# A windowed-attention and expert kernel on one core: feed-forward one slot earlier, a PSUM layout change brought forward, gates moved within their slot, and more loads requested early

## The chip, the cores and the metric

The kernel runs on one core of one Trainium2 chip. The metric is the device time of one execution in microseconds; lower is better. A profile covers one execution, and its span is some 1.7 us shorter than the time of the same execution (221.6 of 223.31). On one core there is no second die to compare with, so a run counts as slow when it is over 1.5% above the fastest run of the same kernel.

## The reference

Eight batches of 576 positions go through attention with eight heads of 64 (four with a plain window of 32 keys, four with every fourth of the last 128 keys). Then each whole batch is sent to one of eight experts, chosen from the mean of its attention output:

```python
pooled = x.mean(axis=1)
logits = pooled @ w_gate
e_idx = np.argmax(logits, axis=1)
...
h = np.maximum(x[mask] @ w1[e], 0.0)
out[mask] = gate_w[mask, None, None] * (h @ w2[e])
```

The expert of a batch, and so the address of its `w1` and `w2` (2 MB each in HBM, 1 MB each as bf16 in SBUF), is known only when all attention of that batch is done.

## The kernel before

Attention is cut into 32 slots, four to a batch. In slot t, PE transposes q or k for a later slot, finishes the attention product (AV) of slot t-1, computes the scores of slot t, and then works off some feed-forward units of an earlier batch. A batch has eight units: four of the first layer (64 matmuls of 128x288 in all, with `w1`), four of the second (32 of 128x512 in all and a tail, with `w2`). `UNITS` says how many units each slot takes:

```python
UNITS = [0] * 6 + [1] * 4 + [2] * 30
```

So the first layer of batch b >= 1 begins in slot 8 + 4b (the lag is 8 slots from the batch's first slot). The gate of batch b is emitted in slot 5 + 4b, when its last AV has been normalised. The gate computes the logits, brings the index of the expert to the POOL engine, and requests weights and later inputs:

```python
def emit_gate(b):
    ...
    nc.vector.max_with_indices(mx[:], mi[:], l_sb[:])
    e_val = nc.values_load(mi[0:1, 0:1].bitcast(I32), engines=[ET.Pool], ...)
    ...                       # three requests for w1, 512 + 256 + 256 KB as landed
    if b == 0:
        load_1(2, GO[0], "q"); load_va(2); load_qb(2)
        load_w2(e_val, w2b)
        load_qa(3); load_vb(2)
    else:
        load_vb(b + 2)
        load_w2(e_val, w2b)
        load_qa(b + 3)
    load_va(b + 3)
    load_qb(b + 3)
```

POOL issues all loads in this order; in the traces of the kernel before never more than eight of the 123 were under way at once. The stores of the output go out from SP. PSUM is laid out in two ways: an early one with two sets of AV banks, and a late one with one AV group `nd` and three banks `m`. The late one began after slot 5. The main loop, cut:

```python
for t in range(6, len(UNITS)):
    if t > 6:
        run_T(t)                       # transposes
    pre.av_a(); flush(); cur.sx()      # AV of t-1, stores, scores of t
    ...
    for i, f in enumerate(items[:k0]):
        f()
        if i == k0 // 2 and gn == 0 and 0 < gb < B:
            emit_gate(gb)              # gate in the middle of the slot
    pre.norm()
    for i, f in enumerate(items[k0:]):
        f()
```

The softmax here doesn't subtract the row's maximum and nothing guards it: scores larger than these inputs give would overflow.

## Time and profile before

| | before |
|---|---|
| time, median of the first three runs | 225.66 us |
| span of the profiled run | 221.6 us |
| PE busy | 194.9 us, 88% |
| share of the software DMA queue | 96.2% |
| gate 7 (its matmul) to the end of the span | 189.27 to 221.6, 32.3 us |

The prediction below shows the lines on which the reading of the bound rests. Where it calls PE cold, it means a slower PE as in this trace: nine transposes took 1.14 us at 33.80, 1.05 us after a wait of 2.22 us had ended, and 0.68 us at 38.42.

### The profile page before, as it was taken

To read this page: it belongs to the slowest core of one execution; us is meant where nothing else is said; L and a number is where in the kernel's file an instruction comes from. 1 tells how busy PE (TensorE), PEld (TensorE's weight loads), DVE (VectorE), ACT (ScalarE), POOL (GpSimd) and SP (SyncE) were. 2 spreads that over 40 slices of the span, in tenths; PEclk is the share of its full clock that TensorE was granted. 3 is DMA by queue.
4 is the path that set the end of the run, shared out by engine and by line. 5 is a ranking of instruction groups with operands and counts; after the bars stand their busy time and mean duration, and the time that the engine had idled before them with its cause. 6 is when DMAs were issued, how large, how long until landed. Compare 5 with 4: busy or idle time off the path is not lost.

```text
span 221.6 us, 8268 instructions
## 1 busy us (share of the span) xinstructions
PE 194.9 (88%) x3570; PEld 135.3 (61%) x3584; DVE 127.9 (58%) x364; ACT 129.9 (59%) x231; POOL 83.1 (38%) x133
## 2 busy tenths in 40 slices
PE   0687559878999999999999999999999999999992
PEld 0565457656567765776577756776577557647641
DVE  5356466657576756765676666676676455415312
ACT  2487666775657766668657665766676755232320
POOL 7974294614852182508450557027100500400000
PEclk9999999999999999999999999999999999999999
DMA  5999499999999999999999999999993699299723
GB/s 81 192 187 188 69 116 193 207 205 180 182 218 203 232 210 215 231 244 209 201 206 232 214 207 229 219 223 208 220 193 109 113 174 288 35 177 249 160 95 118
DMA packets 49925, 41.18 MB, mean 186 GB/s; under 512 B 23777, under 2 KB 38113, under 8 KB 49889
## 3 DMA queue, kind: packets, MB, share of 16 engines
q0 software_dynamic: 43440, 31.20, 96.2%
q1 hardware_dynamic: 6448, 9.46, 12.7%
q8 instruction: 28, 0.46, 0.8%
q14 instruction: 9, 0.07, 0.1%
HBM read 62.41 MB, written 9.44 MB: 324 GB/s over the span
## 4 chain that ended last, share of the span: by engine, by line
PE 60%; DMA 16%; ACT 7%; DVE 5%; issue 5%; POOL 4%; POOLq 1%; SPq 0%
PE m L612 22%; PE m L592 18%; DMA w2b<-in_moe_w_dram 7%; DMA qm<-in_q_dram 7%; PE nd L360 6%; PE m L258 4%; ACT pt L325 3%; PE m L627 3%; ACT qk L279 3%; PE m L268 3%; DMA km<-in_k_dram 3%; DVE pt L332 3%; PE ps L292 2%; DVE ht L599 2%; POOL w1b L538 1%
## 5 line engine op out<-in xcount | busy, mean ns | idle before, releaser
L592 PE MATMUL m<-xt,w1b 128*128 128x288 bf16 x512 | 68.6, 288 | 1.6 <-DVE ht L599 1.6
L592 PEld LDWEIGHTS <-w1b 128*128 128x128 bf16 x512 | 48.6, 98 | 16.3 <-issue 3.0
L612 PE MATMUL m<-w2b,ht 128*128 128x512 bf16 x242 | 56.8, 380 | 1.2 <-DMA w2b<-in_moe_w_dram 0.4
L597 ACT ACTIVATE ht<-m 128x288 bf16<-128x288 f32 x64 | 26.2, 410 | 27.3 <-PE m L592 23.8
L612 PEld LDWEIGHTS <-ht 128*128 128x128 bf16 x256 | 23.9, 98 | 28.2 <-DMA w2b<-in_moe_w_dram 0.5
L332 DVE TENSOR_TENSOR pt<-pt,mk 128x896 bf16<-128x896 bf16 x32 | 20.0, 624 | 28.8 <-ACT pt L325 28.8
L533 POOL DMA_DIRECT2D w1b<-in_moe_w_dram x9 | 6.4, 708 | 74.7 <-PE m L592 57.3
L325 ACT ACTIVATE pt<-ps 128x896 bf16<-128x896 f32 x32 | 28.9, 904 | 6.0 <-PE ps L292 6.0
L497 DVE SCALAR_TENSOR_TENSOR xt<-nd,rd 128x320 bf16<-128x320 f32 (+1 forms) x54 | 27.1, 539 | 7.5 <-ACT rd L470 7.5
L599 DVE TENSOR_SCALAR ht<-m 128x288 bf16<-128x288 f32 x64 | 27.2, 451 | 7.1 <-PE m L592 6.6
L279 ACT ACTIVATE qk<-m 128x512 bf16<-128x512 bf16 (+1 forms) x24 | 17.5, 730 | 16.6 <-PE m L258 13.3
L127 POOL DMA_DIRECT2D vm<-in_v_dram x32 | 24.2, 786 | 2.4 <-DMA qm<-in_q_dram 0.9
L276 DVE COPY qk<-m 128x640 bf16<-128x640 bf16 (+1 forms) x24 | 18.9, 786 | 6.8 <-PE m L258 4.8
L360 PEld LDWEIGHTS <-vm 64*64 64x64 bf16 x896 | 15.9, 114 | 10.7 <-issue 4.4
L470 ACT ACTIVATE rd<-lnd 128x576 f32<-128x576 f32 x32 | 21.8, 682 | 1.0
L360 PE MATMUL nd<-pt,vm 64*64 64x64 bf16 (+1 forms) x760 | 18.0, 194 | 4.3 <-DVE negm L565 2.2
L619 DVE TENSOR_SCALAR osb<-m,gbc 128x512 f32<-128x512 f32 x16 | 12.0, 751 | 16.4 <-PE m L612 16.4
L464 ACT ACTIVATE lnd<-nd 128x576 f32<-128x576 f32 x27 | 17.4, 645 | 4.5 <-PE nd L360 4.4
L292 PE MATMUL ps<-qk 64*64 64x96 bf16 (+3 forms) x608 | 16.1, 213 | 4.4 <-issue 2.0
L292 PEld LDWEIGHTS <-qk 64*64 64x64 bf16 x608 | 15.1, 118 | 4.9 <-issue 3.1
L360 PE MATMUL nd<-pt,ones 64*64 64x256 bf16 (+2 forms) x244 | 16.5, 243 | 0.2 <-issue 0.2
L617 ACT ACTIVATE osb<-m,gbc 128x512 f32<-128x512 f32 x16 | 10.9, 680 | 7.4 <-PE m L612 7.2
(73 smaller groups left out, 210.6 us busy)
## 6 DMA issues: line engine op xcount, KB each, us to landing
w2b<-in_moe_w_dram POOLq DMA_DIRECT2D x8, 1024.0 KB, 13.0
out_dram<-osb SPq DMA_DIRECT2D x32, 256.0 KB, 6.5
km<-in_k_dram POOLq DMA_DIRECT2D x16, 288.0 KB, 12.7
qm<-in_q_dram POOLq DMA_DIRECT2D x16, 288.0 KB, 12.8
w1b<-in_moe_w_dram POOLq DMA_DIRECT2D x16, 256.0 KB, 8.0
w1b<-in_moe_w_dram POOLq DMA_DIRECT2D x7, 512.0 KB, 7.6
vm<-in_v_dram POOLq DMA_DIRECT2D x8, 256.0 KB, 10.7
vm<-in_v_dram POOLq DMA_DIRECT2D x32, 64.0 KB, 8.7
```

The source lines that it names most:

```text
L127: nc.gpsimd.dma_start(out=t[:, h], in_=v[b, h, 0:512, :].rearrange("(c p) d -> p c d", p=P))
L279: nc.scalar.activation(out=ev[x][0], in_=ev[x][1], func=AF.Copy)
L292: nc.tensor.matmul(ps[half(e), a, o : o + rhs.free_size()], lhsT=lhsT, rhs=rhs, start=True, stop=True, skip_group_check=True)
L325: nc.scalar.activation(out=pt[:], in_=s["ps"][:, :, 0:NP], func=AF.Exp, scale=0.125)
L332: nc.vector.tensor_tensor(out=pt[:], in0=pt[:], in1=mk[:, g : g + 1, :].to_broadcast([P, 2, NP]), op=ALU.mult)
L360: x = nc.tensor.matmul(oo, lhsT=lhsT, rhs=rhs, start=start, stop=True, skip_group_check=True)
L470: nc.scalar.activation(out=rd[:], in_=s["lnd", n][:], func=AF.Exp, scale=-1.0)
L497: nc.vector.scalar_tensor_tensor(out=o, in0=a0, scalar=1.0, in1=a1, op0=ALU.mult, op1=ALU.mult, accum_out=s["pool"][:, w, c : c + 1],)
L592: nc.tensor.matmul(hm, lhsT=s["w1"][:, c, fc * P : (fc + 1) * P], rhs=s["xt"][:, c, cols], start=(c == 0), stop=(c == 3))
L597: nc.scalar.activation(out=o, in_=hm, func=AF.Relu)
L599: nc.vector.tensor_scalar_max(out=o, in0=hm, scalar1=0.0)
L612: nc.tensor.matmul(om, lhsT=s["ht"][:, fc, r * P : (r + 1) * P], rhs=s["w2"][:, fc, :], start=(fc == 0), stop=(fc == 7))
```

## The change

The intent is to start feed-forward one slot earlier, so that the whole takes 39 slots instead of 40. To have inputs and banks for it, the late PSUM layout starts with gate 0, and most loads of batch 2 are requested before gate 0. Later gates go to the head of their slot, since they now have one slot less. The core of the diff (the reordering of slots 3 to 5 is cut):

```diff
-UNITS = [0] * 6 + [1] * 4 + [2] * 30
+UNITS = [0] * 5 + [1] * 4 + [2] * 30
...
-    load_tiles(2)
-    load_1(2, GO[0], "k")
+    load_qa(2)
+    load_va(2)
+    load_1(2, GO[1], "k")
...
         if b == 0:
-            load_1(2, GO[0], "q")
-            load_va(2)
-            load_qb(2)
+            load_1(2, GO[1], "q")
             load_w2(e_val, w2b)
...
     emit_gate(0)
-    dve(0)
+    late()
     sl[4].sx()
...
-    for t in range(6, len(UNITS)):
+    for t in range(5, len(UNITS)):
...
+        if gn == 0 and 0 < gb < B:
+            emit_gate(gb)
         pre.av_a()
...
-        for i, f in enumerate(items[:k0]):
+        for f in items[:k0]:
             f()
-            if i == k0 // 2 and gn == 0 and 0 < gb < B:
-                emit_gate(gb)
```

More of the change, by code (lines that the diff above doesn't have):

```diff
@@ L85, in early_bank @@
         return pools["early"].tile([P, 512 if dt == F32 else 1024], dt, name=nm, tag=nm, space=PSUM)[:]
+    for x in range(2):
+        for y in range(3):
+            early_bank(x, y)
     def late():
@@ L737 @@
     dve, act = emit_T(1, a, "k", ((0, 0), (0, 1)))
-    act(0)
+    dve(0)
     act(1)
@@ L741 @@
     dve, act = emit_T(1, a, "q", ((0, 2), (0, 0)))
+    act(0)
     act(1)
     emit_gate(0)
-    dve(0)
+    late()
     sl[4].sx()
-    dve0, act0 = emit_T(1, z, "k", ((1, 1), (1, 2)))
+    run_T(4)
     sl[4].mask()
-    dve0()
-    act0()
-    sl[4].av_a()
-    sl[5].sx()
-    sl[4].av_b()
-    sl[4].ln()
-    sl[4].rd()
-    dve1, act1 = emit_T(1, z, "q", ((1, 0), (1, 1)))
-    sl[5].mask()
-    dve1()
-    act1()
-    sl[4].norm()
     emit_gate_w(0)
-    late()
     def unit(b, u):
@@ L781 @@
         items = [lambda i=i, e=e: i(e) for i, e in zip(items, engs)]
-        if t > 6:
+        gb, gn = divmod(t - 5, NSLOT)
+        if t > 5:
             run_T(t)
+        if gn == 0 and 0 < gb < B:
+            emit_gate(gb)
         pre.av_a()
@@ L786 @@
         cur.sx()
-        if t == 6:
-            run_T(t)
         if pre.on and not cur.on:
@@ L794 @@
         pre.rd()
+        if t == 5:
+            run_T(t)
         k0 = len(items) // 2
-        gb, gn = divmod(t - 5, NSLOT)
-        for i, f in enumerate(items[:k0]):
-            f()
-            if i == k0 // 2 and gn == 0 and 0 < gb < B:
-                emit_gate(gb)
+        for f in items[:k0]:
+            f()
         pre.norm()
-        for i, f in enumerate(items[k0:]):
+        for f in items[k0:]:
             f()
```

## The prediction

> **What bounds the kernel now.** I read the page's busy shares and 40 slices first, then the chain that ended last in order of time, then the timelines of PE and POOL around the two places where that chain leaves PE, and last the busy times of chosen stretches.
>
> ```profile
> PE 194.9 (88%) x3570; PEld 135.3 (61%) x3584; DVE 127.9 (58%) x364; ACT 129.9 (59%) x231; POOL 83.1 (38%) x133
> ...
> PE   0687559878999999999999999999999999999992
> ...
> DMA  5999499999999999999999999999993699299723
> ```
>
> PE is the bound from slice 12 to slice 38 and idles 26.7 us in all (221.6 - 194.9), mostly in the first 12 slices and in the last two. DMA is full nearly everywhere, with one dent near the start (the 4) and dents near the end. These are the two places the change acts on. The busy times of stretches show the first dent:
>
> ```profile
> 24.00:28.00 4.00, 1.72 (x63) 1.50 (x58) 1.99 (x7) 2.28 (x3) 1.69 (x3) 1.00 0.14 15
> 28.00:33.00 5.00, 2.74 (x110) 2.64 (x114) 3.12 (x8) 3.05 (x8) 4.60 (x9) 1.00 0.95 119
> 56.00:168.00 112.00, 108.91 (x2126) 75.24 (x2134) 73.24 (x205) 74.05 (x133) 45.16 (x68) 1.00 1.26 216
> ```
>
> The columns are PE, PEld, DVE, ACT, POOL, clock, DMA share, GB/s. From 24 to 28 us DMA moves 15 GB/s: all requested loads have landed, and nothing more is asked for until gate 0 has picked its expert. From 56 to 168 us PE is busy 108.9 of 112 us while DMA moves 216 GB/s without a hole. So the middle is bound by PE, with DMA only just keeping up.
>
> The first batch, in the timeline:
>
> ```profile
> 26.31 0.70 POOL L533 DMA_DIRECT2D w1b<-in_moe_w_dram  x1 [6.42 <-DVE qk L276]
> ...
> 32.75 0.48 PE L360 MATMUL nd<-pt,vm 64*64 64x64 bf16 x16 [2.22 <-DVE negm L565]
> ...
> 35.49 2.82 PE L592 MATMUL m<-xt,w1b 128*128 128x288 bf16 x16
> ```
>
> The first weights are requested at 26.31. PE waits 2.2 us for the single late `nd` bank group (it has to be freed by slot 4's normalisation, which ended just before `negm`), and feed-forward starts at 35.49. The chain then has four breaks, and these lines show three of them:
>
> ```profile
> 43.51 1.14 issue
> ...
> 48.93 1.98 issue
> ...
> 190.38 0.29 POOLq L527
> ...
> 193.51 15.65 DMA w2b<-in_moe_w_dram
> 209.16 0.05 issue
> 209.21 0.39 PE m L612
> ```
>
> (The fourth is a 0.41 us wait for a q load at 38.41.) The end is the important one: from the gate of batch 7, whose matmul starts at 189.27, through the expert index and the requests, to w2's landing at 209.16 is 19.9 us. PE fills all but 0.39 us of that with other work. The DMA path from gate 7 and PE are in near-perfect balance here: any work taken out of that interval uncovers the transfer.
>
> [...] a w2b load takes 13.0 us in the median and 15.65 at the end, with w1's 1 MB ahead of it. [...] The trace has an instruction queue with 28 packets and 0.46 MB, so 16 KB each, and the two "issue" stalls above are 254 PE instructions apart (counted in the program order). [...] Nine transposes take 1.14 us at 33.8 and 0.68 us at 38.4[...].
>
> **The change, part by part.**
>
> *More early loads.* q, v (with its tail) of batch 2's first head group and k of the second are requested before gate 0: 288 + 256 + 64 + 288 = 896 KB as landed, nearly 2 MB as read. At the 190 GB/s of 8 to 23 us that is 4.7 us of transfer, just the dent of 24 to 28. DMA then runs on from 24 to about 28.5, where w1b's bytes began at 28.2 before. So w1b is late by some 0.3 us, while everything after it arrives about 4.5 us sooner. The q load that PE awaited at 38.41 is one of them: -0.4 us. w2 of batch 0 landed at 48.5 and was used at 55.7, so its earlier arrival is worth nothing.
>
> *Late layout and feed-forward from slot 5.* At 32.75 PE had finished scores 0 to 5, AV 0 to 4 and the transposes up to batch 1. The new order puts the first feed-forward unit directly behind that same work. Its input is w1b's first half. From the waits of POOL's eight request slots I read that this landed between 31.8 and 33.0 (POOL could reuse the first one's slot at 31.8, the third's by 33.0). So PE, done with slot 5's work near 30.6, waits until about 32.7 for weights instead of until 32.75 for `nd`. The wait changes its name and hardly its end. From there both kernels have the same remaining PE work in another order. AV 5, scores 6 and one transpose (2.7 us cold, 32.75 to 35.48) move behind the unit (2.8 us cold): 0.
>
> *Slots 6 to 8.* PE has about 4 us a slot there, and the loop AV, ln, reciprocal, norm, next AV takes the same 3.9 us (39.02 to 42.96 before), so nothing is gained. [...] I keep the 3.1 us of stalls.
>
> *Gates at the slot's head.* With feed-forward one slot further on, the gate is half a slot earlier in its slot, so it has less cover before w1 is used: before, gate 4 at 121.95 to first use at 138.12, 16.2 us; now 16.2 less five feed-forward items (2.6) and some 0.4, 13.2. The third w1b request slot came free 12.2 to 14.0 us after gates 1 to 4. With DMA ahead by 4.5 us while PE is not, I expect landing at 9 to 12 us, no stall; w2 (before 24 us after the gate, now 25 available) neither.
>
> *The end.* Between gate 7 and w2's use there was 19.55 us of PE work (19.94 less 0.39). Moved ahead of the gate are 20 feed-forward matmuls (2.6 us). What is left is gate 0.35, second layer of batch 6 7.0, tail 1.07, first layer of batch 7 8.0, gate weight 0.4: 16.8 us. The DMA path still needs 19.9, perhaps 19.4, because the stores begin 3.4 us sooner relative to the gate and use the idle DMA before w1 moves. So 2.6 to 3.1 us of wait in place of 0.4: +2.2 to +2.7.
>
> Sum of the span: 221.6 - 0.4 + 0.3 + 2.4 = 223.9, a loss of about 1%; as a time, 225.66 x 223.9/221.6 = 228.0.
>
> **Rivals.**
> 1. *A clear gain, 1 to 2%.* Feed-forward a slot earlier, with one slot fewer, might save PE idle time at the start: [...] 3 us go away and the loss at the end is paid back, 221 span, 225. [...]
> 2. *DMA becomes the bound in the middle.* If PE does gain at the start, w1 arrives after 13.2 us and PE stalls at each batch: 0.5 to 1 us in some of them, 229 to 230. For it: 12.2 to 14.0 us before. Against: the filled dent, and DMA's queue was already draining slightly faster than PE used it.
> 3. *The extra loads delay w1b of batch 0.* They are ahead of it in the queue; were they issued late or moved slower than 190 GB/s, w1b lands at 34 to 35 and PE idles, cold, 1 to 2 us more: 229.
> 4. *PE cools at the end.* It would stand for 2.5 us before the last batch's first layer[...].
>
> **Range and chances.** The mechanisms nearly cancel; the largest sure term is the uncovered w2 (+2.4), the largest uncertain one the instruction stalls (-3 to 0). I shade the 228.0 down to 227.3 for rival 1, which has more room than 2 to 4 together. Range 223.5 to 230.0. Faster by 2% needs below 221.1, which would take a gain of over 6 us at the start: 0.06. Slower by 2% is above 230.2, which needs rivals 2 or 3 on top: 0.07.
>
> **What would show it.** Right: DMA without a dent at 24 to 28; PE's first feed-forward matmul near 32.7 and waiting for w1b; no wait for q at slot 7; two "issue" stalls of 1 to 2 us between 40 and 55; PE's work in 56 to 168 unbroken; and at the end a chain from POOL's gate read over w2b to the second layer, with 2.5 to 3 us of PE idle before batch 7's layers. Wrong: an unbroken PE from 32 to 55 (rival 1), waits for w1b in the middle (2), a first feed-forward matmul after 34 (3), or a gate 7 so much earlier that the end comes before 221.

## More of the kernel before

All profiles are of fast runs, and the times quoted for experiments are medians of the fast runs.

One more pair is needed later, from the timeline at the end: the gate's matmul, the first store of batch 6 and the first layer of batch 7 (start, length, engine, line, operation, count).

```profile
189.27 0.34 PE L520 MATMUL m<-wg_t,pooled 128*1 128x8 f32 x8
...
195.06 5.58 SPq L620 DMA_DIRECT2D out_dram<-osb  x4
...
200.52 8.00 PE L592 MATMUL m<-xt,w1b 128*128 128x288 bf16 x64
```

Gate 7 and the first use of its `w1` are 11.25 us apart, and that `w1` landed 11.1 us after the gate, so it was just in time. The stores of batch 6 begin to leave 5.8 us after the gate.

## The result

The changed kernel takes 235.0 us in the median (233.33 to 235.73, four runs) against 225.66 for the kernel before (the three fast runs, 225.33 to 227.25; the fourth, 230.69, is 2.4% above the fastest and counts as slow). The ratio is 1.036 with a 95% interval of 1.027 to 1.045: slower. In the experiments a ratio is the mean time of one kernel's fast runs over that of the other's of the same rounds, so not quite the ratio of the medians quoted; for this result the runs listed would give 1.038, within the interval. The prediction of 227.3, with 223.5 to 230.0 as range, was wrong.

First the page of the changed kernel: PE, clock and DMA in 40 slices of 5.8 us, then the group of the first layer's matmuls (busy us, mean ns, idle time in front of them).

```profile
PE   0487739869999998999899997999999999938992
PEclk9995556979999999999999999999999999997998
DMA  5999999990899999999999999999991996499123
...
L595 PE MATMUL m<-xt,w1b 128*128 128x288 bf16 x512 | 71.5, 298 | 14.5 <-DMA w1b<-in_moe_w_dram 12.1
```

In the kernel before, this group had 68.6 us busy and 1.6 us of idle time before it, none of it for `w1`. Now PE waits 12.1 us for `w1`. There is a 3 near PE's end. The dent in DMA has not gone: it has moved from slice 5 to slice 10. The stretches show it (PE, PEld, DVE, ACT, POOL, clock, DMA share, GB/s):

```profile
24.00:28.00 4.00, 2.28 (x85) 2.07 (x88) 2.24 (x10) 3.05 (x6) 2.23 (x4) 0.50 1.29 200
...
52.00:58.00 6.00, 5.95 (x123) 4.10 (x123) 3.90 (x16) 4.58 (x8) 0.98 (x2) 0.96 0.07 14
```

From 24 to 28 us DMA is full, as intended (200 GB/s, 15 before). But POOL has now issued everything gate 0 allows by 48 us, and until gate 1 has chosen an expert (its matmul at 54.62) there is nothing to ask for: 14 GB/s from 52 to 58.

The chain of waits in the middle repeats the following for batches 2 to 5 (start, length, what):

```profile
79.55 0.29 POOLq L532
...
82.07 9.45 DMA w1b<-in_moe_w_dram
91.52 0.14 issue
91.65 4.08 PE m L595 x32
```

POOL reads the index of the expert of batch 2, requests `w1`, and the first layer starts as soon as it has landed. In the kernel before the chain ran through PE here. The end:

```profile
196.50 0.34 PE L525 MATMUL m<-wg_t,pooled 128*1 128x8 f32 x8
...
198.79 0.71 POOL L538 DMA_DIRECT2D w1b<-in_moe_w_dram  x1 [18.07 <-PE m L615]
199.46 5.58 SPq L623 DMA_DIRECT2D out_dram<-osb  x4
...
209.35 9.67 PE L595 MATMUL m<-xt,w1b 128*128 128x288 bf16 x64 [4.47 <-DMA w1b<-in_moe_w_dram]
```

PE waits 4.5 us for the last `w1`, and the same 64 matmuls then take 9.67 us instead of 8.00, at a clock of 0.5 to 0.57 for the first 3 us.

**Where the 10.1 us of span went (231.7 - 221.6).** I cut at two events: the first matmul of batch 0's second layer, and gate 7. At the cuts the two kernels have done different work, so the kernel before is corrected from its own trace. At the first cut it has done one slot of attention more, 1.57 us (54.12 to 55.69), so 55.62 becomes 54.05. At gate 7 it has still to do 20 first-layer matmuls and a gate weight of batch 6, 2.9 us; with them done first, its gate 7 would stand near 192.1. This is an estimate, good to some tenths.

| part | before, corrected | after | lost |
|---|---|---|---|
| start to second layer of batch 0 | 54.05 | 55.86 | 1.8 |
| from there to gate 7 | 138.05 | 140.64 | 2.6 |
| work moved ahead of gate 7 | 192.1 - 189.27 | | 2.8 |
| gate 7 to the end | 32.35 | 35.2 | 2.85 |

The sum is 10.05. The third line was in the prediction, as 2.6 us; the other 7.2 us were not. The last two lines belong together: in this kernel the end costs 5.7 us.

### The profile page after: what moved, and what is told of

Read it like the earlier page. It is cut to its first block, busy times and chain, and to the rows that moved or that the text cites.

```text
span 231.7 us, 8254 instructions
## 1 busy us (share of the span) xinstructions
PE 196.3 (85%) x3570; PEld 136.6 (59%) x3584; DVE 128.8 (56%) x364; ACT 130.9 (57%) x230; POOL 83.2 (36%) x133
## 3 DMA queue, kind: packets, MB, share of 16 engines
q1 hardware_dynamic: 6448, 9.46, 12.7%
## 4 chain that ended last, share of the span: by engine, by line
PE 42%; DMA 30%; DVE 8%; issue 6%; ACT 6%; POOL 5%; POOLq 2%
PE m L595 24%; DMA w1b<-in_moe_w_dram 23%; PE m L615 9%; DMA vm<-in_v_dram 4%; ACT pt L330 3%; DMA qm<-in_q_dram 3%; PE m L263 3%; DVE pt L337 2%; PE nd L365 2%; ACT qk L284 2%; DVE ht L602 2%; POOL w1b L543 1%; DVE qk L281 1%; PE m L630 1%; POOLq L532 1%
## 5 line engine op out<-in xcount | busy, mean ns | idle before, releaser
L595 PE MATMUL m<-xt,w1b 128*128 128x288 bf16 x512 | 71.5, 298 | 14.5 <-DMA w1b<-in_moe_w_dram 12.1
L595 PEld LDWEIGHTS <-w1b 128*128 128x128 bf16 x512 | 50.5, 101 | 31.7 <-issue 13.0
L502 DVE SCALAR_TENSOR_TENSOR xt<-nd,rd 128x320 bf16<-128x320 f32 (+1 forms) x56 | 28.4, 544 | 7.6 <-ACT rd L475 7.6
L284 ACT ACTIVATE qk<-m 128x576 bf16<-128x576 bf16 (+1 forms) x26 | 19.0, 730 | 13.5 <-PE m L273 8.0
L281 DVE COPY qk<-m 128x576 bf16<-128x576 bf16 (+1 forms) x26 | 20.3, 782 | 9.0 <-PE m L263 8.1
L365 PE MATMUL nd<-pt,vm 64*64 64x64 bf16 (+2 forms) x784 | 18.7, 195 | 3.4 <-issue 2.0
L365 PEld LDWEIGHTS <-vm 64*64 64x64 bf16 x896 | 15.2, 112 | 8.9 <-issue 4.4
L469 ACT ACTIVATE lnd<-nd 128x576 f32<-128x576 f32 x28 | 18.0, 643 | 0.9 <-PE nd L365 0.9
L297 PE MATMUL ps<-qk 64*64 64x96 bf16 (+3 forms) x608 | 15.2, 209 | 2.7 <-issue 1.2
## 6 DMA issues: line engine op xcount, KB each, us to landing
qm<-in_q_dram POOLq DMA_DIRECT2D x16, 288.0 KB, 11.8
```

The costliest lines, as they stand in the source:

```text
L281: nc.vector.tensor_copy(out=ev[x][0], in_=ev[x][1])
L284: nc.scalar.activation(out=ev[x][0], in_=ev[x][1], func=AF.Copy)
L297: nc.tensor.matmul(ps[half(e), a, o : o + rhs.free_size()], lhsT=lhsT, rhs=rhs, start=True, stop=True, skip_group_check=True)
L365: x = nc.tensor.matmul(oo, lhsT=lhsT, rhs=rhs, start=start, stop=True, skip_group_check=True)
L502: nc.vector.scalar_tensor_tensor(out=o, in0=a0, scalar=1.0, in1=a1, op0=ALU.mult, op1=ALU.mult, accum_out=s["pool"][:, w, c : c + 1],)
L595: nc.tensor.matmul(hm, lhsT=s["w1"][:, c, fc * P : (fc + 1) * P], rhs=s["xt"][:, c, cols], start=(c == 0), stop=(c == 3))
```

## The experiments

**Theory 1** is that of cover: the work between a batch's gate and the use of its `w1` has shrunk to about the time that `w1` takes to arrive, so each gate makes PE wait. **Theory 2**: the hole at 52 to 58 us puts the whole DMA stream behind. **Theory 3**: the loss is at the start. All runs are timed against the kernel before on the same chip; the kernel before varied from 224.3 to 231.3 us in those rounds, slow runs included, so I rest on ratios of fast runs and, inside a run, on the trace.

### One slot of lag given back: a_lag8

```diff
-UNITS = [0] * 5 + [1] * 4 + [2] * 30
+UNITS = [0] * 6 + [1] * 4 + [2] * 30
```

> The changed kernel with feed-forward one slot later again (six empty slots), all else of the change kept. Theory 1 (cover): what slows the changed kernel is that w1 of a batch is used about 13 us after its gate, as long as it takes to land, so PE waits for w1 at batches 2 to 5 and 7. With a slot more of cover (some 19 us) no w1 wait is left in the middle or at the end, about 225 to 227 us, level with before. Theory 2 (DMA stream: the hole at 52 to 58 us puts the whole stream behind): waits for w1 or w2 stay, 230 us or more. Theory 3 (the start: early loads in front of the first w1 and a cold PE): about 2 us lost at the start stay, 228 to 229 us.

221.94 us, ratio 0.980 (0.969 to 0.990), on two fast runs only (222.47 and 221.41; the two slow ones took 226.75 and 226.86). No wait for `w1` or `w2` is left, and gate 7 is at 187.53.

```profile
PE   0585669979999999799999999999999999999992
...
L595 PE MATMUL m<-xt,w1b 128*128 128x288 bf16 x512 | 69.4, 291 | 2.1 <-DVE ht L602 1.8
```

With everything else of the change kept, the loss is gone; it hangs on the one slot. By itself this run doesn't separate the theories: the hole at 52 to 58 us is filled too (195 GB/s), and the wait for the first `w1` is gone, as the attention of one more slot now comes before it. The next runs do.

### Gates in the middle of the slot again: a_gatemid

```diff
-        if gn == 0 and 0 < gb < B:
-            emit_gate(gb)
         pre.av_a()
...
+            if i == k0 // 2 and gn == 0 and 0 < gb < B:
+                emit_gate(gb)
```

> The changed kernel with later gates back in the middle of their slot. Theory 1: each gate comes about 2.6 us of PE work later while w1's use stays, so each of batches 1 to 7 waits some 2 to 2.6 us longer: 15 us on top of 235, 248 to 252 us. Theories 2 and 3: the place of the gate in the slot matters little, 234 to 238 us.

264.29 us, ratio 1.164 (1.154 to 1.175): right direction, larger than theory 1 said. `w1` still lands 11.8 to 13.5 us after gates 1 to 7, and PE waits for it at every batch.

```profile
L595 PE MATMUL m<-xt,w1b 128*128 128x288 bf16 x512 | 84.1, 331 | 30.7 <-DMA w1b<-in_moe_w_dram 29.0
...
71.86 6.95 PE L595 MATMUL m<-xt,w1b 128*128 128x288 bf16 x32 [3.60 <-DMA w1b<-in_moe_w_dram]
```

The part I had left out is that PE is slower after a wait. After one of 3.60 us the next 32 matmuls take 6.95 us, where 4.08 is their time in the changed kernel (the chain line above). The group is busy for 84.1 us instead of 71.5: 12.6 us more for the same matmuls.

### Without the early loads: a_noearly

```diff
-    load_qa(2)
-    load_va(2)
-    load_1(2, GO[1], "k")
+    load_tiles(2)
+    load_1(2, GO[0], "k")
```

(and gate 0 requests the rest again, as before.)

> The changed kernel without the 2 MB of early loads (only k of batch 2 before gate 0, as in before). Theory 1: first feed-forward matmul near 32.7 instead of 34.5, then the q wait of before comes back; the w1 waits of the middle and the end stay: 232 to 235 us. Theory 2: the hole at 52 to 58 us goes, w1 lands in time in the middle, 228 us or less. Theory 3: most of the loss goes, 228 us or less.

233.99 us, ratio 1.033 (1.027 to 1.040), as theory 1 said. The hole is back at 24 to 28 us (26 GB/s), and 52 to 58 us has 171 GB/s. The first feed-forward matmul comes at 33.31, the second layer of batch 0 at 53.21, 2.65 us earlier than in the changed kernel. And yet gate 7 is at 196.63, where it was at 196.50: PE now waits for `w1` at batches 1 to 6 as well (14.8 us in all with batches 0 and 7). So what is gained at the start is taken back at the gates: theory 3 falls as the main cause. And with no hole at 52 to 58 us the waits for `w1` are still there: theory 2 falls.

### The early loads alone: b_early

The same lines of the diff, put into the kernel before.

> The kernel before with the early loads alone. Theory 1: 16 us of cover remain, so no w1 wait; first w1 lands 1 to 2 us later, but feed-forward started at 35.5 anyway, and the q wait of 0.4 us goes: 225 to 227 us, same. Theory 2: a hole in the DMA stream near 50 to 58 us and waits for w1 or w2 afterwards, 229 us or more. Theory 3: 1.5 to 2 us lost at the start, 228 us.

223.93 us, ratio 0.991 (0.980 to 1.001). The hole moves to 50 to 56 us (71 GB/s) here too, and the middle has no wait for weights after it. One wait of 0.61 us for `w1` appears at gate 7 (189.34 to 201.16, so `w1` landed 11.7 us after the gate): the kernel before had its 11.25 us of cover there with nothing to spare. A hole without waits in the middle speaks against theory 2 once more.

### The gates' place alone: b_head

The gate moved to the head of the slot in the kernel before.

> The kernel before with gates 1 to 7 at the head of their slot, alone. Theory 1: cover grows from 16.2 to some 19 us, nothing waited for w1 before, and the last w2 gets about 3 us more, so only its 0.4 us wait goes: 225 to 226.5 us, same. If the head itself cost something (a wait of PE for the gate's bank or for the pooled sums, 7 times), 1 to 3 us slower, 228 us.

225.08 us, ratio 0.991 (0.981 to 1.001); no wait for weights anywhere. The head of the slot costs nothing that can be seen.

### Weights that don't wait for the gate: a_w1free

The loads of gates 1 to 7 take a fixed expert, so POOL requests them without waiting:

```diff
+        if gn == 3 and gb + 1 < B:
+            emit_gate_loads(gb + 1, gb + 1)     # w1, w2 of expert gb + 1, same bytes, same order
```

> Wrong result on purpose: the changed kernel with the loads of gates 1 to 7 taken for a fixed expert, so that they no longer wait for the gate and follow in the queue at once. Same bytes, same order. Theory 1: no wait for w1 is left in the middle or at the end, no hole at 52 to 58 us; what stays is the late start: 225 to 228 us. If the sheer rate of DMA were the limit, waits for weights stay and the time stays above 231 us.

226.66 us, ratio 1.006 (0.995 to 1.017). Its output is wrong, which doesn't matter for the time. The sheer rate of DMA is not the limit: the same bytes in the same order need no wait when they are asked for in time. Against the changed kernel's trace the span falls by 8.9 us (231.7 to 222.8): 1.6 up to the second layer of batch 0, 1.45 in the middle (140.64 to 139.19), and 5.8 from gate 7 to the end (35.2 to 29.4). The 1.6 are not the edit's: it leaves the loads of gate 0 as they were, and gate 0 alone came 1.0 us sooner in this trace (23.45). So most of the loss is at the last gate, not in the waits of the middle, though those add up to 3.7 us (0.82, 0.86, 1.48, 0.51).

### Loads held back so that w1 goes first: a_prio and b_prio

```diff
         else:
+            load_qb(b + 2)
             load_vb(b + 2)
             load_w2(e_val, w2b)
             load_qa(b + 3)
         load_va(b + 3)
-        load_qb(b + 3)
```

> The changed kernel with the last two loads of each gate (k and q of the second head group, 576 KB) held back until the next gate's w1 has been requested. Theory 1: w1 lands some 2.5 to 3 us sooner after its gate (10 to 11 us instead of 13.3), the waits for w1 at batches 2 to 5 go, the end stays: 230 to 232 us. If the stream's rate is the limit, waits for other loads take their place, 234 us or more.

233.92 us, ratio 1.034 (1.026 to 1.042): a miss. Of the four waits for `w1` in the middle one is left (1.09 us) and a wait for `w2` joins it (0.74), yet the stretch from the second layer of batch 0 to gate 7 is as long as in the changed kernel: 140.44 us. In the middle `w1` landed 12.0 to 13.4 us after its gate, against 12.8 to 13.7, so the order of the queue is worth less than the 2.5 to 3 us that I expected. POOL now runs dry sooner (48 GB/s from 46 to 56 us), and the end, with 4.50 us of wait, is untouched.

> The kernel before with the same two loads held back. w1 had cover to spare there: theory 1 says no gain, 225 to 227 us; a loss of 1 to 3 us if DMA runs dry at gates, since the held-back loads filled it.

227.2 us, ratio 1.004 (0.995 to 1.013): no gain, as expected.

### The stores and the last w1: a_storelate

What was open by now: at the last gate nothing else is queued, and still `w1` takes 12.7 us (196.50 to 209.22). In the changed kernel the second layer of batch 6 follows right behind the gate, so its stores leave 3.0 us after it instead of 5.8. Here those stores wait until PE has begun batch 7's first layer:

```diff
-        flush()
+        hold["on"] = t in (34, 35)
+        flush()                      # does nothing while on
...
         for f in items[:k0]:
             f()
+            if t == 35 and stores:
+                flush(hold["last"])  # stores depend on that matmul
```

> The changed kernel with the six stores of batch 6 held until PE has begun batch 7's first layer, that is until w1 of batch 7 has landed. If the stores that leave at 199 to 206 us delay that w1 (12.8 us after its gate though the queue was empty), it lands some 2.5 to 3 us sooner, about 10 us after the gate, PE waits 1.5 us instead of 4.5 and does not cool, and the run is 3 to 4.5 us shorter than the changed kernel: 230 to 232 us. If those 12.8 us are the request's own path, nothing changes: 234 to 236 us.

231.95 us, ratio 1.027 (1.022 to 1.033). The timeline:

```profile
198.05 0.35 PE L525 MATMUL m<-wg_t,pooled 128*1 128x8 f32 x8
...
208.40 8.00 PE L595 MATMUL m<-xt,w1b 128*128 128x288 bf16 x64 [1.97 <-DMA w1b<-in_moe_w_dram]
```

`w1` lands 10.2 us after the gate (2.5 sooner), PE waits 1.97 us, and the layer takes 8.00 us. From gate 7 to the end it is now 31.05 us instead of 35.2: 4.15 us less, within what was expected. That gate 7 came 1.5 us later in this run (198.05) hides part of it in the time.

The packets in the two traces, counted by queue, say how. In the changed kernel, from 203.5 to 209.2 us, the queue of the loads and that of the stores moved 124 GB/s each; with the stores held back the loads alone moved 194 (203 to 208.2). The other traces agree in the main: the last `w1` landed 12.6 to 12.8 us after gate 7 where the first store left up to 3.0 us after it (the changed kernel, a_gatemid, a_noearly, a_prio, a_fill), 11.1 to 11.7 where it left after 5.8 (the kernel before, b_early, b_prio, a_lag8mid), and 10.1 to 11.8 where it left after 7.3 (a_lag8, a_lag8_again, b_head).

### PE kept busy through the wait: a_fill

Twenty matmuls of no use, into a bank that nobody reads, ahead of batch 7's first layer:

```diff
+        if t == 35:
+            fill = bank()
+            for j in range(20):
+                nc.tensor.matmul(fill, lhsT=st[6]["ht"][:, j % 8, 0:P], rhs=st[6]["w2"][:, j % 8, :], ...)
```

> The changed kernel with 20 matmuls of no use (128x512, some 0.22 us each, into a bank that nobody reads) where PE waits for the last w1. If the slow clock after that wait cost 1.7 us (9.67 us for the 64 matmuls of batch 7's first layer, 8.0 before), the layer takes 8.0 us and the run is 1.5 to 1.8 us shorter: 233 us. If the layer was slow for another reason, say the loading of w2 next to it, it stays at 9.7 us and the time at 235.

232.74 us, ratio 1.031 (1.025 to 1.037).

```profile
205.65 4.49 PE L793 MATMUL m<-w2b,ht 128*128 128x512 bf16 x19
210.16 8.00 PE L595 MATMUL m<-xt,w1b 128*128 128x288 bf16 x64
```

The layer takes 8.00 us again, and gate 7 to the end falls from 35.2 to 33.5 us. The slow clock after the wait (0.52 over the first 3 us of the layer in the changed kernel, 1.00 here from 210 to 212) cost 1.7 us; it was not the loading of `w2` beside it.

### The old lag, gates in the middle: a_lag8mid, and a_lag8_again

> The changed kernel at the old lag (six empty slots) and with gates in the middle of their slot again: only the late layout from gate 0 and the early loads are left of the change. By the theory of cover it has the 16 us of the kernel before, no wait for w1, 222 to 226 us, level with a_lag8 within 1%. If the place of the gate is what made a_lag8 fast, it is 2 to 3 us slower than that.

223.23 us, ratio 0.988 (0.983 to 0.994). It has the 0.35 us wait for `w2` at the end that the kernel before has, and no other for weights.

> The a_lag8 kernel again, with five rounds, as the version that may beat both: 0.98 of the kernel before again, within 0.01, if the first three rounds were no accident; 0.99 to 1.0 if they were.

224.01 us in five fast runs, ratio 0.989 (0.985 to 0.994). The 0.980 of the first three rounds rested on two fast runs; 0.989 is between what the two expectations named, and its interval lies below 1. So the two versions with the late layout and the early loads at the old lag are the fastest, about 1.1% faster than the kernel before, and the place of the gate makes no clear difference between them.

## Why the prediction was wrong

**The early loads.** The dent at 24 to 28 us is filled, as predicted. That w1b would be "late by some 0.3 us" was too little: the first feed-forward matmul comes at 34.46, against 33.31 without the early loads. That is 1.15 us by this pair, in which gate 0 stands at 24.45 and 24.46. Over all traces the first half of `w1` landed 8.7 to 9.0 us after gate 0 in the four without the early loads and 8.7 to 10.2 in the ten with them, so the size varies. What failed is the next sentence, "everything after it arrives about 4.5 us sooner". It holds only up to gate 1. Then POOL has no request to make, and the head start is lost in a new hole of 6 us.

**"I expect landing at 9 to 12 us, no stall."** This is the step that failed in the middle. It supposed that `w1` is slow only because of the loads ahead of it, and set aside the 12.2 to 14.0 us that the kernel before had shown. Measured at batches 2 to 5, `w1` landed 13.1, 13.1, 13.7 and 12.8 us after its gate (each wait's end less the gate, less the 0.14 us of issue), much as in the kernel before (12.4 to 13.5 at the same batches). The cover was too large by 0.8 us as well: PE came to the first layer 12.4 us after the gate each time, not 13.2. The gate, the landing and the 64 first-layer matmuls with their two slots of attention make a loop that sets the pace, since gate b+1 follows them directly. Rival 2 of the prediction described these waits of 0.5 to 1 us; I gave it too little weight, and tied it to a gain at the start that didn't come. The waits cost less than their sum of 3.7 us: 1.45 us by a_w1free. The other 1.1 us of the middle's 2.6 stay there in a_w1free. They are not waits, as PE idles no longer there than in the kernel before (3.6 us against 3.5); their cause stays open.

**The end.** This is the step that cost most, 5.7 of the 10.05 us. The prediction set PE's work against `w2` alone: "The DMA path still needs 19.9, perhaps 19.4". That length was about right, as the last `w2` landed at 215.53, 19.0 us after gate 7. But PE has to get past `w1` first, and the prediction didn't weigh that wait. In the kernel before, the last `w1` landed 11.1 us after the gate and PE came to it at 11.25. With the work moved ahead of the gate PE comes after 8.4 us, and `w1` landed after 12.7: a wait of 4.47 us, and `w2` was there when PE came to it at 219.3. The prediction also said that the stores would help by leaving sooner. They left sooner (3.0 us after the gate instead of 5.8) and did harm: `w1` landed 1.6 us later than in the kernel before, and 2.5 later than with the stores held back (a_storelate). And PE's clock was slow after the wait of 4.47 us, at 0.50 to 0.57 for 3 us: rival 4, which I named and left out of the sum, cost 1.7 us (a_fill). Together 4.47 + 1.7, less the 0.4 us wait for `w2` that is gone, make the 5.7 us. The term of 2.6 us of first-layer work moved ahead of the gate was right.

**The start.** The exchange of one wait for another ("The wait changes its name and hardly its end") is what happened, but 1.8 us later than 32.7: PE waited 3.96 us for `w1`, to 34.46. Of the 1.8 us, 0.6 are a later gate 0 (24.45 against 23.81) and 1.0 a slower landing; this is rival 3. The "issue" stalls (1.14 and 1.98 us before), which I kept at 3.1 us in all as an estimate, came as one of 1.99 us at 47.56 and none of that size 254 PE instructions later; from 49.55 to 52.5 us the clock was 0.51, and 16 matmuls took 2.93 us, against 2.39 at 40.07, so part of the saving was lost to a slow clock.

**The range.** I added the rivals as alternatives of 1 to 2 us each. They were parts of one loop and came together: late first weights, waits at gates, a wait at the end, and its clock.

## What to carry to other kernels

Where an address is computed, count the work between the moment it is known and the first use of what it fetches, and compare it with the whole path measured in the trace: chain, request, transfer, and whatever else leaves at that time. If the two are about equal, a slot taken out to shorten a schedule comes back as waits at such points. Do it for each transfer that a gate starts, the first one used before all: here the last gate alone cost 5.7 of 10 us, and the transfer that the prediction had weighed there was not the one that PE waited for. A transfer that is slow in a full queue need not be fast in an empty one, as stores can meet it there (here the last `w1` landed 12.7 us after its gate with the stores beside it, 10.2 us without them); look for a place in the trace where it is alone before you rely on that.

## What else the traces show

- **The last `w1` alone and beside stores.** With no other load ahead and the stores held back (a_storelate), the three requests of `w1` (1 MB as landed, 2 MB as read) took 7.9 us from the first issue (200.34) to the landing (208.26); with the stores beside them (the changed kernel) 10.4 us (198.79 to 209.22).
- **PE after a wait.** After 20 waits of PE for `w1` of 0.5 to 2.0 us (batches 1 to 7) the next 32 matmuls took 4.08 or 4.09 us; after ten waits of 2.75 to 6.1 us they took 5.46 to 6.97. So in these traces waits of 2.75 and 2.90 us were enough for a slow PE, and one gap cost 1.4 to 2.9 us. For the "issue" stalls the length alone did not decide: after one of 1.98 us in the kernel before the next 8 first-layer matmuls took 1.15 us, after one of 1.99 in the changed kernel the next 16 took 2.93.
- **The "issue" stalls.** In the traces of the two kernels PE stood still for 1.14, 1.98 and 1.99 us where no semaphore explains it. Their cause is not shown. But in every trace PE's stalls of this kind over 0.4 us, from 29 us on, came at much the same counts of recorded PE instructions (weight loads included), whatever the kernel: near 955, 1463 and 1718, and a few later ones, at distances of about 254 or a multiple of it.
- **The recorded clock at the beginning.** The kernel before shows full clock from the start (1.00 from 0 to 24 us), the changed one 0.50 from 24 to 33 us, but the same first-layer matmuls and transposes were slow in both: before, under a recorded clock of 1.00, nine transposes took 1.14 us at 33.80 (0.68 at 38.42) and the first 16 first-layer matmuls 2.82 us; in the changed kernel the latter took 4.00 us at 0.50, and nine transposes 0.92 us at 38.25 (0.67 at 42.30). The mean clocks of the two pages (0.999 and 0.937) are therefore not a comparison of the kernels.
